# A retention block with a gated MLP on one core: two bit operations per float64 tile, a new order, and four half loads on ScalarE's queue

## The chip, the cores and the metric

The kernel runs on one core of a Trainium2 chip. The metric is the time of one execution on the device in microseconds. One core has a matrix engine (TensorE, PE in the profile, with its weight loads as PEld), three elementwise engines (VectorE as DVE, ScalarE as ACT, GpSimd as POOL), and a queue engine (SyncE, SP) that only issues transfers. Each engine runs its own instructions in program order; engines wait for one another and for transfers by semaphores. Transfers of all queues run on the core's 16 DMA engines.

## The reference

There are 4 batches, 8 heads, 768 positions and a head width of 64. The first part is retention, a linear attention with a decaying state, the second a gated MLP with a spatial gate:

```python
for t in range(S):
    state = gamma[None, :, None, None] * state + np.einsum('bhd,bhe->bhde', k[:, :, t], v[:, :, t])
    y[:, :, t] = scale * np.einsum('bhd,bhde->bhe', q[:, :, t], state)
# x: y with the heads side by side, [B, 768, 512]
h = x @ w_in                                             # [B, 768, 1024]
h = 0.5 * h * (1.0 + np.tanh(c * (h + 0.044715 * h ** 3)))
u, v = h[..., :512], h[..., 512:]
v_n = (v - mean(v)) / sqrt(var(v) + 1e-6) * g_ln
v_s = np.einsum('ts,bsd->btd', w_sg, v_n) + b_sg[None, :, None]
out = x + (u * v_s) @ w_out
```

`w_in` and `w_out` arrive as float64, all else as float32.

## The kernel before, in words

**Tiles and stages.** Positions are split in two halves of 384, each in six chunks of 64; heads go in four pairs. One attention unit (batch, half, pair) is written as three digits: 012 is batch 0, half 1, pair 2. There are 32 units. The MLP part runs on blocks of a batch and a half. Its matrix products are done in three passes of float32 in a reduced form: each operand is split into a high part and the rest, and high x high, high x rest and rest x high are summed.

**The order is written out by hand.** `PROG` is a string of some 1,200 words; a loop at the end reads it from left to right, and each word emits the instructions of one step. The order in which an engine sees its instructions is the order of the words that have work for it. The first letter names the step, digits its unit, and a last letter D, G or A the engine where there is a choice (VectorE, GpSimd, ScalarE). The steps that matter here:

- Attention: L loads a unit (`a_load`), P scales keys, S computes scores, D the states of the chunks, T scans the states (VectorE), M masks the scores (VectorE), W copies states beside them, K carries a state out and C carries it into the second half, O computes the output, X multiplies it out of PSUM (VectorE), H and I split it in a high part and the rest.
- MLP: V (four parts per block of 128 positions) and U (two parts) are the products with the two halves of `w_in`, v and u their activations; s and N (`v_rstd`, twelve small VectorE operations) make the normalization, n, a, b apply and split; G (three parts) is the product with `w_sg`, e (line 434) takes it out of PSUM, m gates, h and j split; Y is the product with `w_out`, r and y add the residual and store.
- Weights: a word with v, u, o or s and a number is a step for one of four tiles of `w_in`'s second half (v), of its first half (u), of `w_out` (o), or for one of twelve of `w_sg` (s). l loads. For the twelve float64 tiles (v, u, o), k (ScalarE) and b (VectorE) make a float32 from the upper 32-bit words, r (ScalarE) scales the lower words, a (GpSimd) adds them; h and o split the result.
- `~40` emits 40 filler matmuls on PE whose result nobody reads; R builds a table; Q loads the gate constants.

**Queues.** Every load and store goes through SP's queue except the first table, which ScalarE issues. An attention unit is three transfers: the keys (line 238, 384 KB on 128 partitions) and two halves of queries and values (line 247, 192 KB each, one on partitions 0 to 63, one on 64 to 127). A load waits until its buffer is free; the buffers of the units 000 to 003 are used for the first time there. Line 240 leaves out the second half for units that are in `ON_ACT`; a word Z (`a_load_rest`, line 249) then issues it from ScalarE's queue. `ON_ACT` is made of the Z words of `PROG` (line 106), and in the order before there is none.

**PSUM.** Two pools of four banks: one for attention (ds, sc, po), one for the MLP (pv, pu, ps, py, and the fillers). A matmul group that opens a tile waits until a bank of its pool has been read out.

Of the kernel before, what the change touches and what calls it, by code (L numbers as in the profile page):

```python
# [53 lines left out]
U0011 ko0 n001 a000 n002 U0031 bo0 a001 ko2 U0021 hs3A bo2 hs11A O013 u003 hs1A os3D D100 hs10A X013 b000G
u002 D101 H013A T100 S100 hs4A b001G hs2A S101 u001 M100 L102 ko1 K100 V0120 ko3 ao2 M101 V0110 L103 ro1 V0121
hs8A I013D a002 os1D V0111 Q hs6A os10D V0122 hs7A b002D W1001A U0101 os7D os4D P102A V0123 bo1 u010 V0112
v012 os8D V0100 W1000A s012 os2G V0113 T101 P103A V0101 ao1 v011 U0110 W1011A s011 K101 ho1A ao0 V0102 W1010A
U0120 os11D os6D V0103 bo3 U0130 v010 s010 ho0G U0121 N01 U0131 oo1G u012 U0111 u013 n011 n012 O100 u011 n010
ao3 D102 a010 X100 a011 O101 T102 H100A b010G D103 a012 ho2A S102 b012D S103 b011D L110 I100D G0020 M103 ho3G
L111 G0000 X101 C110 oo0G M102 C111 G0021 oo3D G0001 H101G G0022 P110A oo2D G0002 I101G V1020 K102 e000 W1021G  # L60
G0010 P111A m000D V1021 W1020G h000 G0011 j000D T103 r000G V1000 G0012 W1031A K103 W1030G V1001 e001 e002 O102
m001G D110 X102 m002G h001 O103 T110 D111 H102G h002 S110 W1100A j001D S111 W1101G M110 L112 G0030 M111 j002G
C113 L113 G0110 T111 I102G C112 G0031 W1110A r001D X103 r002G W1111A V1022 V1002 H103G G0032 P112G G0111 e003
I103D Y0000 m003G P113A V1023 h003 r003G V1003 v102 j003G G0112 s102 v100 s100 Y0001 G0100 y000 G0120 G0101
G0121 G0102 G0122 e010 e011 U1000 m010D m011D Y0010 r010D r011G U1001 G0130 u100 Y0020 Y0011 Y0021 y001 V1010
y002 G0131 Y0030 G0132 h010 h011 j010D Y0031 j011G e012 V1011 m012G y003 Y0110 e013 h012 r012G Y0130 j012D
Y0100 m013G V1012 h013 r013G O110 j013D D112 X110 O111 H110G T112 D113 S112 W1120A I110D S113 X111 W1121A L200
M112 H111A Y0111 I111G M113 L201 Y0131 y011 T113 Y0101 y013 W1131G Y0120 y010 W1130G V1013 Y0121 P200G v101
# [516 lines left out]
```

## Time and profile before

| | us |
|---|---|
| time, median of 3 runs | 412.82 (412.26 to 413.41) |
| the profiled execution's own time | 414.86 |
| its span, first to last instruction | 413.1 |
| busy: PE / PEld | 400.7 / 366.1 |
| busy: DVE / ACT / POOL | 247.1 / 146.6 / 155.2 |
| HBM read / written | 34.48 MB / 6.29 MB |

Times of the trace count from the first instruction. In rows of the timeline the first number is the start, the second the length, both in us; x24 is the number of instructions merged; brackets tell how long the engine idled before and what released it. In rows by line the busy time in us and the mean of one in ns follow the first bar, the idle time before and its releasers the second. A wait row is "engine line <- engine line waited for: us in total, times, longest us".

### The profile page before, as it was taken

To read this page: it belongs to the slowest core of one execution; us is meant where nothing else is said; L and a number is where in the kernel's file an instruction comes from. 1 tells how busy PE (TensorE), PEld (TensorE's weight loads), DVE (VectorE), ACT (ScalarE), POOL (GpSimd) and SP (SyncE) were. 2 spreads that over 40 slices of the span, in tenths; PEclk is the share of its full clock that TensorE was granted. 3 is DMA by queue.
4 is the path that set the end of the run, shared out by engine and by line. 5 is a ranking of instruction groups with operands and counts; after the bars stand their busy time and mean duration, and the time that the engine had idled before them with its cause. 6 is when DMAs were issued, how large, how long until landed. Compare 5 with 4: busy or idle time off the path is not lost.

```text
span 413.1 us, 9386 instructions
## 1 busy us (share of the span) xinstructions
PE 400.7 (97%) x3937; PEld 366.1 (89%) x3940; DVE 247.1 (60%) x488; ACT 146.6 (35%) x266; POOL 155.2 (38%) x161
## 2 busy tenths in 40 slices
PE   8998997999999999999999899999999999999996
PEld 3657886989999998999999898899998999899996
DVE  2799899987632674672761492741746855262652
ACT  4597687623411223442121152430234312230010
POOL 3446533638721530341651154230544133302421
PEclk9999999999999999999999999999999999999999
DMA  7999785032501070514042042500243210000012
GB/s 236 289 311 251 247 299 190 6 90 66 155 19 40 21 229 1 155 27 129 2 129 82 2 141 89 152 22 2 73 141 102 72 59 21 2 0 2 0 58 96
DMA packets 18123, 41.39 MB, mean 100 GB/s; under 512 B 2464, under 2 KB 8096, under 8 KB 18080
## 3 DMA queue, kind: packets, MB, share of 16 engines
q1 hardware_dynamic: 17936, 40.51, 32.6%
q8 instruction: 31, 0.51, 0.5%
q10 hardware_dynamic: 144, 0.27, 0.2%
q14 instruction: 12, 0.10, 0.1%
HBM read 34.48 MB, written 6.29 MB: 99 GB/s over the span
## 4 chain that ended last, share of the span: by engine, by line
PE 78%; DVE 9%; DMA 9%; issue 1%; ACT 1%; SPq 0%; ACTq 0%
PE ps L424 24%; PE py L462 16%; PE pv L351 13%; PE pu L407 13%; PE po L319 5%; DMA mw<-in_qv_dram 5%; PE sc L278 4%; PE ds L270 4%; DMA raw<-in_w_v_dram 2%; DMA tab<-in_c_tab_dram 1%; DMA raw<-in_w_sg_dram 1%; DVE ws L223 1%; DVE st L365 1%; DVE wx L187 1%; DVE mw L296 1%
## 5 line engine op out<-in xcount | busy, mean ns | idle before, releaser
L424 PE MATMUL ps<-ws,vh 128*128 128x384 f32 x576 | 105.7, 336 | 0.0
L424 PEld LDWEIGHTS ps<-ws,vh 128*128 128x128 f32 x576 | 100.6, 188 | 1.6
L407 PE MATMUL pu<-xh,wu 128*128 128x384 f32 x384 | 73.0, 339 | 1.6 <-DVE gt L434 1.1
L351 PE MATMUL pv<-wv,xh 128*128 128x512 f32 x288 | 74.1, 396 | 0.0
L462 PE MATMUL py<-gh,wo 128*128 128x384 f32 x384 | 72.1, 336 | 0.0
L407 PEld LDWEIGHTS pu<-xh,wu 128*128 128x128 f32 x384 | 67.5, 188 | 3.8 <-DVE gt L434 1.4
L462 PEld LDWEIGHTS py<-gh,wo 128*128 128x128 f32 x384 | 67.0, 188 | 0.7
L351 PEld LDWEIGHTS pv<-wv,xh 128*128 128x128 f32 x288 | 53.2, 188 | 9.5
L148 ACT COPY mw<-sq 64x320 f32<-64x320 f32 (+1 forms) x44 | 36.2, 822 | 29.9 <-DVE sq L283 29.6
L434 DVE SCALAR_TENSOR_TENSOR gt<-ps,gb 128x384 f32<-128x384 f32 x32 | 19.3, 612 | 43.8 <-PE ps L424 43.7
L449 ACT CAST gh<-gt 128x384 fp32r<-128x384 f32 x32 | 16.4, 514 | 74.5 <-POOL gt L445 31.3
L296 DVE TENSOR_TENSOR mw<-sc,tab 64x384 f32<-64x384 f32 x64 | 35.5, 555 | 9.4 <-PE sc L278 7.9
L365 DVE BATCH_NORM_STATS2 st<-v 128x6 f32<-128x512 f32 x24 | 16.4, 683 | 31.4 <-ACT v L361 31.4
L473 POOL TENSOR_TENSOR o<-xh 128x384 f32<-128x384 f32 x16 | 18.0, 1125 | 40.6 <-DVE gt L445 40.3
L326 DVE TENSOR_TENSOR x<-po,tab 128x384 f32<-128x384 f32 x32 | 17.6, 549 | 25.0 <-PE po L319 20.4
L278 PE MATMUL sc<-mw,kt 64*64 64x64 f32 x768 | 27.4, 219 | 5.1 <-DVE x L326 3.6
L477 DVE TENSOR_TENSOR o<-py,o 128x384 f32<-128x384 f32 x32 | 17.4, 552 | 25.0 <-PE py L462 24.9
L278 PEld LDWEIGHTS sc<-mw,kt 64*64 64x64 f32 x768 | 24.7, 135 | 8.0 <-DVE x L326 3.9
L283 DVE TENSOR_TENSOR_SCAN sq<-step,ds 128x384 f32<-128x384 f32 x32 | 30.1, 941 | 2.3 <-PE ds L270 1.6
L319 PEld LDWEIGHTS po<-mw 128*64 128x64 f32 (+1 forms) x768 | 26.2, 137 | 5.8 <-issue 3.7
L445 POOL TENSOR_TENSOR gt<-gt,u 128x384 f32<-128x384 f32 x18 | 19.2, 1071 | 31.7 <-DVE gt L434 31.7
L319 PE MATMUL po<-mw 128*64 128x64 f32 (+1 forms) x768 | 31.0, 226 | 0.0
(61 smaller groups left out, 420.2 us busy)
## 6 DMA issues: line engine op xcount, KB each, us to landing
kt<-in_kk_dram SPq DMA_DIRECT2D x32, 384.0 KB, 5.3
mw<-in_qv_dram SPq DMA_DIRECT2D x64, 192.0 KB, 5.3
out_dram<-o SPq DMA_DIRECT2D x32, 192.0 KB, 1.8
raw<-in_w_sg_dram SPq DMA_DIRECT2D x12, 192.0 KB, 7.2
raw<-in_w_v_dram SPq DMA_DIRECT2D x4, 512.0 KB, 7.2
raw<-in_w_u_dram SPq DMA_DIRECT2D x4, 512.0 KB, 8.6
raw<-in_w_out_dram SPq DMA_DIRECT2D x4, 512.0 KB, 7.6
gb<-in_gb_dram SPq DMA_DIRECT2D x1, 386.0 KB, 4.5
```

The source lines that it names most:

```text
L148: nc.scalar.copy(out=out, in_=in_)
L278: mm(out=scs[u][o, c], lhsT=kt[i, c], rhs=mv[j][i, c], start=True, stop=True)
L283: nc.vector.tensor_tensor_scan(out=sqs[u].rearrange("p e c -> p (e c)"), data0=step_t[:, p].rearrange("p e c -> p (e c)"), data1=dss.pop(u ...
L296: nc.vector.tensor_tensor(out=mv[j][h], in0=sc[h], in1=mask_t[h, p : p + 1, :].to_broadcast([64, NCH, C]), op=ALU.mult,)
L319: mm(out=pos[u][o, c], lhsT=w[j][i, c], rhs=mv[j][i, c], start=True, stop=True)
L351: mm(out=pv[b, hf, k], lhsT=x[:, p, a, k * 128 : (k + 1) * 128], rhs=wv_t[:, w, p], start=(p == 0 and n == 0), stop=(p == NP - 1 and n == 2),)
L365: nc.vector.bn_stats(out=st, in_=vt[b, hf, k])
L407: mm(out=pu[b, hf, f], lhsT=wu_t[:, w, f, p * 128 : (p + 1) * 128], rhs=x[:, p, a], start=(n == 0), stop=(n == 11),)
L424: mm(out=ps[b, hf, d], lhsT=vh[b, t][:, v, d * 128 : (d + 1) * 128], rhs=ws_t[hf * NT + t][:, w], start=(n == 0), stop=(n == 3 * NT - 1),)
L434: nc.vector.scalar_tensor_tensor(out=t, in0=ps.pop((b, hf, d)), scalar=g_t[:, d : d + 1], in1=b_t[:, hf * HT : (hf + 1) * HT], op0=ALU.mul ...
L445: engines[e].tensor_tensor(out=t, in0=t, in1=ut.pop((b, hf, d)), op=ALU.mult)
L462: mm(out=py[b, hf, c], lhsT=wo_t[c][:, w, d * 128 : (d + 1) * 128], rhs=gh[b, hf, d][:, a], start=(d == 0 and n == 0), stop=(d == 3 and n ...
```

## The change

The bits of a float64 are taken in another way. Before, k took the absolute value of the upper word read as a float32; b limited it from below (line 183), masked and shifted it left by three (line 184), and set the two upper bits from the original (line 187). After, k multiplies the upper word, read as a float32, by 2^-112, which moves its exponent; b shifts left by three and sets the sign bit from the original. Two VectorE operations stand where three stood, for each of the twelve tiles.

The order is written anew as a whole. It holds the same steps, apart from the fillers (40, 9, 8, 1 and 10 before; 40, 5, 3, 7, 1 and 1 after) and four new words Z000 to Z003. Some steps that have a choice move to another engine, in both directions. The beginning of the string and the places around N20:

```diff
-~40 lv0 R lv2 L000 lv3 L001 rv0 kv2 rv2 bv2 L010 kv0 bv0 P000A lu2 S000 av2 D000 M000 kv3 ~9 av0 rv3 T000 L011
-hv2A W0000A bv3 hv0A lv1 S001 P001A ov0D W0001A D001 ls10 ov2G M001 O000 lu0 av3 X000 P010A lu3 S010 H000A ~8
-K000 hv3A M010 ku2 ov3G T001 ru2 L002 C010 bu2 D010 W0011A ~1 P011A S011 I000D W0010A K001 L003 V0000 au2 M011
-C011 kv1 V0010 rv1 T010 V0020 hu2A bv1 W0100A D011 O001 ku0 ou2D L012 ~10 ru0 bu0 ru3 ku3 X001 av1 W0101A L013
-P002A S002 T011 H001G hv1A D002 M002 W0111A au0 O010 ls0 W0110A I001D hu0A S003 lo3 ov1D P003A O011 X010 ou0G
-lu1 T002 H010A D003 I010G M003 W0020A U0000 W0021A bu3 V0001 P012A V0021 X011 K002 au3 V0011 C012 T003 H011A
-P013A S012 W0030A I011D O002 W0031G M012 hu3A D012 ro3 K003 S013 X002 L100 C013 ou3D H002A O003 ku1 T012 I002G
+~40 L000 lv2 L001 lv3 lv0 lu2 R Z000 L010 kv2 rv2 bv2 Z001 av2 rv3 hv2A ov2D kv0 L011 rv0 bv0 ku2 kv3 P000G
+S000 L002 ru2 bu2 D000 ~5 bv3 lo3 T000 av0 P010A lu0 S010 P001A lu3 M000 S001 av3 W0000A D001 lv1 M010 hv0A ~3
+W0001A au2 M001 hv3A L003 O000 P011A K000 S011 ov3D C010 D010 T001 hu2G ~7 Z002 ov0G M011 W0011A W0010A X000
+K001 L012 ou2D ro3 O001 C011 T010 H000A D011 ku0 ~1 I000D ru0 bu0 V0000 ru3 V0010 W0100A X001 W0101G ls0 V0020
+H001A au0 T011 rv1 O010 L013 kv1 ~1 I001D ku3 S002 bv1 Z003 W0111A X010 W0110G M002 P002A av1 O011 H010A hu0A
+D002 P012A bu3 S012 hv1A S003 ls7 P003A ov1D lu1 T002 I010G V0011 Q ls3 V0001 M012 W0020A au3 V0021 W0021A
+X011 K002 M003 P013A D003 H011G hu3A O002 ou0G C012 T003 D012 ku1 S013 I011D L100 ru1 ou3D U0000 W0031A X002
...
-V2022 V2001 P213G V2023 V2002 v202 G1121 s202 U2000 V2003 U2001 v200 s200 U2010 u200 V2010 U2011 V2011 u201
-G1122 V2012 G1110 V2013 G1111 v201 s201 Y1030 N20 G1112 h110 j110G Y1031 e111 n202 U2020 e112 m111D O210 m112D
+G1120 s200 G1131 P213A G1110 G1132 G1111 V2010 G1112 V2011 e111 G1121 m111G V2012 r111D G1122 V2013 Y1030 v201
+s201 U2020 h110 h111 N20 j110G Y1031 j111G U2021 e112 O210 u202 e113 m112G D212 y103 O211 X210 m113G h112 T212
...
-    def w_abs(m, i):
+    def w_scale(m, i):
         hf = raw[m, i].bitcast(F32).rearrange("p (n t) -> p n t", t=2)[:, :, 1]
         x = wx[m, i] = act.tile([128, DF], F32, tag="gh", name="wx", bufs=4)
-        nc.scalar.activation(out=x, in_=hf, func=AF.Abs)
+        nc.scalar.activation(out=x, in_=hf, func=AF.Copy, scale=2.0**-112)
 
     def w_bits(m, i):
         hi = raw[m, i].bitcast(I32).rearrange("p (n t) -> p n t", t=2)[:, :, 1]
-        x = wx[m, i]
-        xi = x.bitcast(I32)
-        nc.vector.tensor_scalar(out=x, in0=x, scalar1=2.0**-15, scalar2=None, op0=ALU.max)
-        nc.vector.tensor_scalar(
-            out=xi, in0=xi, scalar1=0x07FFFFFF, scalar2=3, op0=ALU.bitwise_and, op1=ALU.logical_shift_left
-        )
+        xi = wx[m, i].bitcast(I32)
+        nc.vector.tensor_scalar(out=xi, in0=xi, scalar1=3, scalar2=None, op0=ALU.logical_shift_left)
         nc.vector.scalar_tensor_tensor(
-            out=xi, in0=hi, scalar=-0x40000000, in1=xi, op0=ALU.bitwise_and, op1=ALU.bitwise_or
+            out=xi, in0=hi, scalar=-0x80000000, in1=xi, op0=ALU.bitwise_and, op1=ALU.bitwise_or
         )
```

More of the change, by code (lines that the diff above doesn't have):

```diff
@@ L54 @@
[L54 to L68, printed above, removed]
@@ new lines @@
+ko2 os3D ls5 v001 V0023 bo2 v000 U0010 ls10 v002 s001 os0G H012A U0020 ro2 ls8 s002 I012G P101A U0100 s000
+W0130A ao2 U0030 N00 ko1 W0131G U0011 ko3 ro1 U0031 ko0 hs11G hs1A n000 U0021 u001 n001 a000 n002 a001 O013
+os1D a002 b000D D100 hs10A X013 b001G D101 hs5A T100 u003 S100 u002 H013G ro0 S101 b002D L102 W1000A os5D
+V0120 bo1 W1001A V0110 L103 bo0 V0121 V0111 ls2 bo3 V0122 M100 K100 V0112 I013G V0100 T101 os10G P102A V0123
+M101 W1011A U0101 K101 ao1 v012 V0113 W1010A s012 V0101 u010 os11G v011 U0110 ho1A s011 hs2G hs4A V0102 oo1G
@@ new lines @@
+hs8A hs6A U0120 hs7A os8D P103A V0103 os2D os7D U0130 v010 os6D os4G s010 U0121 N01 ao0 U0131 u012 ao3 U0111
+ho0A u013 O100 u011 n011 ho2A n012 D102 n010 O101 X100 ho3G a010 T102 D103 a011 oo2G a012 S102 H100A b012D
+S103 W1021A L110 b011D G0020 I100D M102 b010G L111 V1020 G0000 X101 C111 oo0G M103 C110 H101A G0021 I101D oo3G
+G0001 P110A G0022 K102 W1020G V1021 T103 G0002 W1031A K103 G0010 e000 P111A m000G W1030A G0030 r000D h000
+G0011 j000G G0031 G0012 G0032 e001 e002 m001G V1000 G0110 m002D h001 r001D h002 V1001 j001D j002G e003 G0111
@@ new lines @@
+O110 j012D D112 e013 O111 X110 m013G D113 T112 H110A S112 I110G h013 S113 M112 L200 j013G V1120 X111 W1120G
+U1021 L201 M113 H111A W1121G Y0110 u102 I111D r012D V1121 T113 r013G U1030 W1130A W1131G Y0111 P200A V1100
+y011 U1031 V1110 u103 P201A V1101 V1111 U1100 O112 D200 X112 O113 H112A T200 D201 I112G W2001A S200 K200 X113
+W2000A S201 M200 L202 H113A V1122 I113G T201 V1102 L203 M201 V1123 W2011A K201 V1103 W2010A V1112 v112 v110
+s112 Y0130 s110 V1113 P202A Y0120 v111 s111 Y0131 N11 Y0121 P203A Y0100 U1101 y013 n110 n111 Y0101 a110 n112
@@ new lines @@
+O301 H300A T302 D303 I300G W3020A S302 W3021G X301 S303 M302 L310 H301A K302 I301G G2000 C310 T303 C311 L311
+V3000 M303 W3030A W3031G G2001 K303 V3010 G2002 V3011 e200 P310G G2030 m200D h200 r200G G2010 j200D G2031
+P311G V3001 G2032 G2011 O302 D310 X302 O303 H302G T310 D311 I302D S310 W3100G X303 S311 M310 L312 H303A W3101G
+V3012 C313 I303G M311 C312 G2012 L313 T311 V3013 e201 V3002 W3110G v301 G2020 m201G s301 G2100 W3111G h201
+P312A j201D G2021 r201G V3003 G2022 v300 s300 P313A Y2020 e202 G2101 e203 m202G Y2030 m203D h202 r202D h203
@@ new lines @@
+Y2000 j202D j203G G2102 r203G Y2021 e210 m210G Y2031 y202 r210G Y2001 y203 Y2010 y200 G2110 h210 j210G Y2011
+G2120 y201 G2130 G2121 G2131 G2122 G2132 G2111 V3020 G2112 V3021 e211 e212 O310 m211G D312 X310 h211 r211G
+O311 T312 D313 H310G S312 W3121A m212D I310D S313 h212 r212D W3120A X311 j211G V3022 M313 H311A U3000 j212G
+T313 Y2130 I311D W3130A e213 W3131G V3023 M312 Y2120 m213G v302 s302 Y2100 h213 r213G N30 U3001 j213G O312
+u300 O313 n302 X312 Y2131 n301 H312A n300 Y2101 I312G y213 a300 a301 Y2121 b300D a302 X313 b301G V3120 y210
@@ L105 @@
+Y3021 Y3031 y302 r310D U3130 y303 G3112 U3131 e311 m311G G3120 u313 r311G Y3000 G3121 Y3010 G3122 h310 h311
+j310G Y3011 j311D Y3001 e312 e313 m312G Y3110 y301 y300 m313G h312 Y3130 j312D h313 Y3120 r312G Y3100 j313D
+r313D Y3111 Y3131 y311 Y3121 y313 Y3101 y312 y310
 """.split()
```

64 lines of the change are left out of this document (26 added, 38 removed).

## The prediction

> **What bounds the kernel now.** First the granted clock and the page's busy line, then three stretches of the span, cut at two matmul groups that stand in both orders: the scores of unit 012 (step S012) and the first product with the spatial weights (step G0020).
>
> ```profile
> core 0: 413.1 us, clock 1.000
> ...
> PE 400.7 (97%) x3937; PEld 366.1 (89%) x3940; DVE 247.1 (60%) x488; ACT 146.6 (35%) x266; POOL 155.2 (38%) x161
> ...
> 12.62:40.95 28.33, 25.80 (x427) 19.37 (x429) 25.54 (x43) 22.42 (x39) 15.01 (x15) 1.00 1.04 278
> 40.95:89.05 48.10, 44.00 (x569) 39.23 (x568) 43.54 (x91) 31.99 (x62) 21.16 (x22) 1.00 0.50 163
> 89.05:413.10 324.05, 319.47 (x2908) 303.04 (x2904) 173.75 (x348) 86.90 (x159) 114.29 (x117) 1.00 0.23 69
> ...
> 12.62 0.92 PE L278 MATMUL sc<-mw,kt 64*64 64x64 f32 x24
> ...
> 40.95 0.92 PE L278 MATMUL sc<-mw,kt 64*64 64x64 f32 x24
> ...
> 89.05 6.51 PE L424 MATMUL ps<-ws,vh 128*128 128x384 f32 x36
> ...
> 399.75 9.87 PE L462 MATMUL py<-gh,wo 128*128 128x384 f32 x56
> ```
>
> A window's row gives its length, then the busy time of PE, weight loads, DVE, ACT and POOL, clock, DMA share and GB/s. PE is the engine to shorten, at full clock. The last stretch has 4.58 us without a matmul, of which 3.48 lie behind the last one (399.75 + 9.87 = 409.62, to 413.10); 1.1 is a stall. So what can be won lies in the first 89 us: 2.53 us idle in the first stretch, 4.10 in the second, and the filler matmuls in front of expected waits. What ends those waits is told by the waits of PE, and by DVE ahead of the longest one:
>
> ```profile
> PE sc L278 <- DVE x L326: 3.6, 2, 2.9
> PE sc L278 <- DMA mw<-in_qv_dram: 1.3, 3, 0.5
> ...
> PE pu L407 <- DVE gt L434: 1.1, 1, 1.1
> PE pu L407 <- ACT v L361: 0.5, 1, 0.5
> ...
> 7.88:89.05 81.17, 73.05 (x140) 1.00 0.72 210
> ...
> 60.19 0.42 DVE L183 TENSOR_SCALAR wx<-wx 128x512 f32<-128x512 f32 x1
> ...
> 63.64 0.41 DVE L183 TENSOR_SCALAR wx<-wx 128x512 f32<-128x512 f32 x1
> ...
> 65.62 0.55 DVE L326 TENSOR_TENSOR x<-po,tab 128x384 f32<-128x384 f32 x1
> ...
> 66.23 0.91 PE L278 MATMUL sc<-mw,kt 64*64 64x64 f32 x24 [2.91 <-DVE x L326]
> ```
>
> DVE is 90% busy from its first weight operation to G0020 (73.05 of 81.17), and PE's longest stall, 2.91 us, ends on a DVE multiply that stood behind the bit operations of two weight units. In the first stretch the DMA engines are full instead (share 1.04), and PE waits for units to land.
>
> **The two operations.** Twelve weight units pass through these groups:
>
> ```profile
> L196 ACT ACTIVATE raw<-raw 128x512 int32<-128x512 uint32 x12 | 8.1, 672 | 6.7 <-DMA raw<-in_w_out_dram 3.6 <-DMA raw<-in_w_v_dram 3.0
> L175 ACT ACTIVATE wx<-raw 128x512 f32<-128x512 f32 x12 | 7.9, 668 | 3.3 <-DMA raw<-in_w_v_dram 3.3
> ...
> L183 DVE TENSOR_SCALAR wx<-wx 128x512 f32<-128x512 f32 x12 | 7.3, 611 | 6.8 <-ACT wx L175 6.8
> L184 DVE TENSOR_SCALAR wx<-wx 128x512 int32<-128x512 int32 x12 | 7.1, 588 | 0.4
> ```
>
> Line 183 goes: 12 x 0.611 = 7.3 us of DVE, all of it ahead of G0020, where DVE is the fullest engine. Line 184 loses one of its two steps. The page has no single-step shift; its nearest rows are 588 ns with two steps and 611 with one, so I take no change, with 12 x 0.02 us either way. ScalarE's Abs (668 ns) becomes a Copy with a scale, which line 196 already is (672): +0.05 us in all, taken as nothing, since ACT has 5.9 of 28.33 us free even in the fullest stretch.
>
> **The loads.** The second halves of units 000 to 003 move to ScalarE's queue. The unit that sets S012 lands late in a stretch of full DMA engines:
>
> ```profile
> kt<-in_kk_dram SPq DMA_DIRECT2D x32, 384.0 KB, 5.3
> mw<-in_qv_dram SPq DMA_DIRECT2D x64, 192.0 KB, 5.3
> ...
> raw<-in_w_u_dram SPq DMA_DIRECT2D x4, 512.0 KB, 8.6
> ...
> 23.00:26.90 3.90, 3.88 (x43) 2.85 (x43) 3.48 (x7) 3.41 (x7) 1.50 (x1) 1.00 1.03 412
> 27.00:36.00 9.00, 7.33 (x146) 5.43 (x144) 8.71 (x14) 7.87 (x13) 4.56 (x4) 1.00 1.05 237
> ...
> 0.72 0.40 ACTq L481 DMA_DIRECT2D tab<-in_c_tab_dram  x1
> ...
> 28.49 2.00 SPq L247 DMA_DIRECT2D mw<-in_qv_dram  x2
> ...
> DMA to landing us min/median/max: 8.3/8.7/9.0
> ```
>
> The last row is the landing of the two issues at 28.49, the halves of unit 012: the second, issued at about 30.0, is down 9.0 us later, at 39.0. The issue order puts weights into the first of the two DMA windows (412 GB/s) and attention units into the second (237 GB/s), and half of a unit's bytes goes to 64 partitions at a time (lines 245 to 247). Counting sizes in issue order, unit 012 is complete on SP after 9152 KB before and 9280 after; the latter holds 320 KB more of weights and leaves out the half of 003 that stands behind it in ScalarE's order. That is 0.8 us more (320 KB at 412 GB/s) and 0.8 less (192 KB at 237), so 39.0 again, if the other queue changes nothing. The three halves that are issued from ScalarE ahead of that point are worth 0.83 us each (192 KB at 237 GB/s) if they run beside other traffic: 2.5 us, and 36.5. I take 36.5, because the engines have shown 412 GB/s on full-width traffic and a stream that mixes both partition halves is nearer to that than one half after the other; 39.0 stays as the other end.
>
> The Trainium skill speaks against me: SBUF — State Buffer, section "Can I just issue two DMAs to hit both halves?", says that two concurrent transfers to the two partition halves serialize on the same 16 engines, with a gain of only 6%. The 237 GB/s row agrees with slow halves in one queue; no run here shows them in two. By that rule S012 stays at 39.0, the first rival's case.
>
> What else ScalarE pays: four issues of 0.40 us, by the table's row, 1.6 us, covered by those 5.9 idle us; without that cover they cost 1.6 us. SP is passed the other way: its queue now begins with unit 000, with the weights v0 behind two more units' starts, covered by the 40 fillers that hold PE until 12.62 in both.
>
> **The order.** Ahead of S012 stand 17 fillers besides the first 40 instead of 28, and five groups of work go behind it: the scores and states of 003, one half of a U group and three V groups.
>
> ```profile
> 28.42 2.11 PE L492 MATMUL wp<-warm 128*128 128x512 bf16 x9 [0.16 <-issue]
> ...
> 35.09 0.91 PE sc L278 x22
> ...
> 36.85 0.84 PE ds L270 x24
> 37.69 1.24 PE pu L407 x6
> 38.93 2.09 PE pv L351 x9
> ```
>
> The moved groups are 0.91 + 0.84 + 1.24 + 2.09 = 5.1 us. Ten fillers (one record is missing) take 2.11 us, so 11 fewer are 2.3 us. PE's own work up to S012 shrinks from 25.80 to 25.80 - 5.1 - 2.3 = 18.4 us; it could be there at 31.0 with no wait, at 33.5 with the waits of before (2.53). Landing at 36.5 comes later and decides. The fillers are thus no gain by themselves: they are wait of another name.
>
> From S012 to G0020 PE has 44.00 + 5.1 = 49.1 us of work. Of the 4.1 us idle there, 3.6 ended on DVE; five of the twelve weight units lie in this part (5 x 0.611 = 3.05 us less on DVE), so 0.55 of it stays, with the 0.5 that ended on ACT: 1.1. G0020 then comes at 36.5 + 49.1 + 1.1 = 86.7 instead of 89.05: 2.35 us.
>
> Behind G0020 the matmuls are the same. The 1.1 us stall stands at N20:
>
> ```profile
> 233.06 0.17 DVE L375 TENSOR_SCALAR lna<-mvar 128x3 f32<-128x3 f32 x1
> ...
> 236.01 0.61 DVE L434 SCALAR_TENSOR_TENSOR gt<-ps,gb 128x384 f32<-128x384 f32 x1
> ...
> 236.68 1.31 PE L407 MATMUL pu<-xh,wu 128*128 128x384 f32 x6 [1.10 <-DVE gt L434]
> ```
>
> Line 434 waits behind the twelve small operations of N20 (233.06 to 236.01), and a U group for the bank that it frees. The new order puts U2020 and that release ahead of N20, with the next new bank six attention groups later. I take the 1.1 us as won and no new stall; if another stall of its kind opens, nothing is won, and this is the unknown cost, 0 to 2.2 us.
>
> Sum: 413.1 - 2.35 - 1.1 = 409.65 of span. The profiled execution took 414.86 us; the median is 2.04 lower, at 412.82. Taken from it: 412.82 - 3.45 = 409.4.
>
> **Rivals.** (1) The halves serialize in two queues as in one. S012 at 39.0, G0020 at 39.0 + 49.1 + 1.1 = 89.2, nothing won in front, 1.1 behind: 411.9. For it: DMA share 1.04, full already. Against: the 237 beside 412 GB/s.
>
> (2) DVE alone sets the front. Then its 7.3 us come out whole, 8.4 with N20: 404.4. For it: 73.05 of 81.17 us busy; S012 could be reached at 31.0, and loads that land by 33 would show it. Against: before S012 DMA is full and PE's waits there end on landings.
>
> (3) Slower: Z003 is late. In ScalarE's order this issue stands behind both activations of weight v1, whose load is complete after 7744 KB. Before, unit 002 was complete after 7616 KB, and its scores waited for the landing until 31.73:
>
> ```profile
> 31.73 0.85 PE L278 MATMUL sc<-mw,kt 64*64 64x64 f32 x21 [0.46 <-DMA mw<-in_qv_dram]
> ```
>
> So v1 lands near 32, and with three activations of 0.67 Z003 is issued at 34. If it lands as slowly as SP's halves (9.0), S003 waits until 43, and behind it are 49.1 - 0.9 us of PE work: G0020 at 43 + 48.2 + 1.1 = 92.3, 3.2 later, less 1.1: 414.9. It decides from a landing 5.7 us behind the issue (39.75 + 49.3 = 89.05). For it: the in-order queue. Against: SP's 9.0 us contain its own backlog, and ScalarE's queue has none.
>
> (4) The new order gains nothing from fewer DVE operations, as PE finds other waits: between (1) and 412.8, held in (1).
>
> **Chances.** Forecast 0.48, own range 407.4 to 411.3; (1) 0.17; (2) 0.20; (3) 0.15. About 0.3%, 1.2 us, is what a measurement can tell from no change. Faster: 0.47 of the forecast, all of (2) and 0.06 of (1), 0.73; same: 0.01, 0.10 of (1) and 0.03 of (3), 0.14; slower: 0.13. The range reaches near (2) and half way into (3): 404.8 to 413.6.
>
> **What would show it.** DVE 5 to 8 us less busy, with two groups of 12 on the weights' bits; 57 fillers; S012 near 36.5 with a DMA landing as its releaser, G0020 near 86.7; no PE wait of 2 us on DVE; under 4 us without a matmul behind G0020. Wrong: S012 at 39 or later (rival 1), S003 released by a half on ScalarE's queue (rival 3), or a stall of over 2 us behind G0020, which no step here foresees.

## The result, and the profile after

The changed kernel takes 425.53 us (median of 4 executions, 422.18 to 427.13) against 413.12 us (412.26 to 414.95): 1.0249 of before, 95% interval 1.0204 to 1.0294. It is slower by 10 to 12 us where 3.4 us less was forecast. Its profiled execution took 426.16 us, with a span of 424.2.

The busy line and the granted clock on the page of the changed kernel:

```profile
PE 404.1 (95%) x3925; PEld 368.9 (87%) x3929; DVE 248.8 (59%) x472; ACT 144.5 (34%) x267; POOL 158.8 (37%) x164
...
PEclk9989799998999999999999999999999999999999
```

DVE has 16 instructions fewer (472 for 488) and is busy 1.7 us longer (248.8 for 247.1). The clock, full throughout before, dips in three places. The stretches of the changed kernel, cut at the same two steps, and three tens with a dip:

```profile
12.49:37.20 24.71, 19.31 (x352) 14.84 (x355) 21.13 (x34) 17.86 (x33) 11.90 (x12) 0.93 1.04 290
37.20:97.77 60.57, 52.45 (x638) 46.19 (x634) 50.11 (x92) 35.51 (x67) 32.93 (x33) 0.92 0.47 139
97.77:424.20 326.43, 321.06 (x2906) 303.47 (x2904) 176.17 (x344) 87.95 (x164) 108.59 (x111) 1.00 0.22 69
...
20.00:30.00 10.00, 8.49 (x150) 6.21 (x148) 9.82 (x16) 7.65 (x15) 5.52 (x7) 0.83 1.04 320
...
40.00:50.00 10.00, 6.84 (x83) 5.61 (x85) 3.93 (x7) 3.99 (x7) 2.02 (x3) 0.66 0.44 131
...
90.00:100.00 10.00, 6.88 (x116) 6.05 (x112) 9.19 (x20) 2.83 (x5) 5.59 (x5) 0.83 0.22 70
```

The first stretch ends 3.75 us earlier than before (37.20 for 40.95). The second is 12.47 us longer (60.57 for 48.10), the third 2.38 (326.43 for 324.05): 11.1 us of span in all. Single microseconds inside these dips show 0.50, so a mean of 0.66 over 10 us means that some 6.8 us of them ran at half clock, 0.83 means 3.4 us. PE around those dips:

```profile
17.92 0.30 PE L276 MATMUL sc<-mw,kt 64*64 64x64 f32 x2 [2.62 <-DMA mw<-in_qv_dram]
...
36.44 0.92 PE L268 MATMUL ds<-mw,kt 64*64 64x64 f32 x24
37.20 1.17 PE L276 MATMUL sc<-mw,kt 64*64 64x64 f32 x26
43.16 1.54 PE L276 MATMUL sc<-mw,kt 64*64 64x64 f32 x22 [4.79 <-DMA mw<-in_qv_dram]
44.63 3.60 PE L349 MATMUL pv<-wv,xh 128*128 128x512 f32 x9
...
95.08 2.76 PE L276 MATMUL sc<-mw,kt 64*64 64x64 f32 x48 [3.05 <-DVE x L324]
97.77 1.70 PE L422 MATMUL ps<-ws,vh 128*128 128x384 f32 x6
...
100.40 0.50 PE L349 MATMUL pv<-wv,xh 128*128 128x512 f32 x1 [0.47 <-DVE xh L336]
```

S012 (37.20; the 26 matmuls are its 24 and the first two of S003) follows the states ahead of it without a wait. Right behind it PE waits 4.79 us for unit 003, and the nine V matmuls behind that wait take 3.60 us, where the prediction's row has 2.09. At 95.08 the scores S102 wait 3.05 us for a bank that DVE empties. The first of the two ends on the half that ScalarE issues; ScalarE's timeline:

```profile
32.21 1.25 ACT L178 ACTIVATE wx<-raw 128x512 f32<-128x512 f32 x2
34.17 0.47 ACTq L245 DMA_DIRECT2D mw<-in_qv_dram  x1
```

and the landing of that one issue (its size in KB, then us to landing):

```profile
mw<-in_qv_dram ACTq DMA_DIRECT2D x1, 192.0 KB, 8.9
```

34.17 + 8.9 = 43.07: the first score of S003 begins at 43.16. The second wait has DVE in front of it, first on four splits of spatial weights, then on N01 (89.69 to 93.10), its scalings, and only then the multiply X100 that empties the bank:

```profile
83.43 5.41 DVE L221 TENSOR_TENSOR ws<-raw,ws 128x384 fp32r<-128x384 f32 x4 [0.43 <-ACT ws L149]
...
89.69 1.21 DVE L373 TENSOR_SCALAR lna<-mvar 128x3 f32<-128x3 f32 x1
...
93.10 1.46 DVE L385 TENSOR_SCALAR v<-v,mvar,lny 128x512 f32<-128x512 f32 x3
94.47 0.55 DVE L324 TENSOR_TENSOR x<-po,tab 128x384 f32<-128x384 f32 x1
```

The four splits take 1.35 us each. GpSimd works beside them, on its timeline:

```profile
83.91 1.33 POOL L221 TENSOR_TENSOR ws<-raw,ws 128x384 fp32r<-128x384 f32 x1
85.20 3.23 POOL L200 TENSOR_TENSOR wx<-wx,raw 128x512 int32<-128x512 int32 x2
```

DVE's groups show where its saving went:

```profile
L336 DVE TENSOR_TENSOR xh<-x,xh 128x384 fp32r<-128x384 f32 x15 | 11.9, 792 | 0.0
...
L185 DVE SCALAR_TENSOR_TENSOR wx<-raw,wx 128x512 int32<-128x512 int32 x12 | 9.4, 782 | 0.4
...
L221 DVE TENSOR_TENSOR ws<-raw,ws 128x384 fp32r<-128x384 f32 x8 | 7.7, 993 | 0.4 <-ACT ws L149 0.4
L184 DVE TENSOR_SCALAR wx<-wx 128x512 int32<-128x512 int32 x12 | 7.0, 586 | 9.2 <-ACT wx L178 9.2
```

The weights' bits are two groups of 12 now. Before, the same splits of xh took 559 ns each (14 of them) and those of the spatial weights 741 (9); here 792 and 993. In these two groups alone DVE is busy 5.4 us longer than before (11.9 for 7.8 and 7.7 for 6.4), of the 7.3 us saved.

### The profile page after: what moved, and what is told of

It reads as the page before. It is cut to its first block, busy times and chain, and to the rows that moved or that the text cites. A ratio compares the mean times of both kernels' runs of the same rounds, so it can differ in the third digit from the quotient of the medians.

```text
span 424.2 us, 9359 instructions
## 1 busy us (share of the span) xinstructions
PE 404.1 (95%) x3925; PEld 368.9 (87%) x3929; DVE 248.8 (59%) x472; ACT 144.5 (34%) x267; POOL 158.8 (37%) x164
## 4 chain that ended last, share of the span: by engine, by line
PE 75%; DVE 11%; DMA 10%; issue 2%; ACT 2%; SPq 0%; DVEq 0%; ACTq 0%
PE ps L422 22%; PE py L460 15%; PE pv L349 13%; PE pu L405 12%; DMA mw<-in_qv_dram 8%; PE po L317 5%; PE ds L268 4%; PE sc L276 4%; DVE ws L221 2%; DMA raw<-in_w_v_dram 1%; DVE vh L395 1%; DVE v L385 1%; DVE xh L336 1%; DVE st L363 1%; DVE sq L281 1%
## 5 line engine op out<-in xcount | busy, mean ns | idle before, releaser
L422 PE MATMUL ps<-ws,vh 128*128 128x384 f32 x576 | 107.3, 337 | 0.0
L349 PE MATMUL pv<-wv,xh 128*128 128x512 f32 x288 | 78.5, 404 | 0.5 <-DVE xh L336 0.5
L405 PE MATMUL pu<-xh,wu 128*128 128x384 f32 x384 | 74.6, 339 | 0.8 <-DVE gt L432 0.5
L460 PEld LDWEIGHTS py<-gh,wo 128*128 128x128 f32 x384 | 67.1, 188 | 2.4 <-DVE gt L432 1.3
L349 PEld LDWEIGHTS pv<-wv,xh 128*128 128x128 f32 x288 | 53.7, 191 | 10.4 <-DVE xh L336 1.4
L443 POOL TENSOR_TENSOR gt<-gt,u 128x384 f32<-128x384 f32 x20 | 20.5, 1033 | 81.9 <-DVE gt L432 81.8
L149 ACT COPY mw<-sq 64x320 f32<-64x320 f32 (+1 forms) x41 | 33.0, 806 | 35.4 <-DVE sq L281 33.9
L276 PE MATMUL sc<-mw,kt 64*64 64x64 f32 x768 | 28.5, 228 | 10.9 <-DMA mw<-in_qv_dram 7.9
L276 PEld LDWEIGHTS sc<-mw,kt 64*64 64x64 f32 x768 | 26.1, 142 | 12.7 <-DMA mw<-in_qv_dram 5.5
L415 ACT ACTIVATE u<-pu 128x384 f32<-128x384 f32 x32 | 15.6, 491 | 58.4 <-PE pu L405 58.3
L336 POOL TENSOR_TENSOR xh<-x,xh 128x384 fp32r<-128x384 f32 x17 | 17.7, 1041 | 45.1 <-ACT xh L149 44.5
L324 DVE TENSOR_TENSOR x<-po,tab 128x384 f32<-128x384 f32 x32 | 17.6, 549 | 24.5 <-PE po L317 22.1
L151 POOL COPY mw<-sq 64x384 f32<-64x384 f32 (+1 forms) x23 | 21.2, 922 | 24.6 <-DVE sq L281 12.5
```

The costliest lines, as they stand in the source:

```text
L149: nc.scalar.copy(out=out, in_=in_)
L151: engines[e].tensor_copy(out=out, in_=in_)
L276: mm(out=scs[u][o, c], lhsT=kt[i, c], rhs=mv[j][i, c], start=True, stop=True)
L336: engines[e].tensor_tensor(out=t[:, p, 1], in0=xs.pop((b, hf, p)), in1=t[:, p, 0].bitcast(F32), op=ALU.subtract)
L349: mm(out=pv[b, hf, k], lhsT=x[:, p, a, k * 128 : (k + 1) * 128], rhs=wv_t[:, w, p], start=(p == 0 and n == 0), stop=(p == NP - 1 and n == 2),)
L405: mm(out=pu[b, hf, f], lhsT=wu_t[:, w, f, p * 128 : (p + 1) * 128], rhs=x[:, p, a], start=(n == 0), stop=(n == 11),)
```

## The experiments

Ratios are to the kernel before, run beside each on the same chip (medians there 414.15 to 414.8 us). G0020 and the rest are the profiled execution's: where the first product with the spatial weights begins, and the span from there. The diffs show the words around each move; the rest of a line is left out.

| | edit | median us | ratio [95%] | G0020 / rest |
|---|---|---|---|---|
| after | | 425.53 | 1.0249 [1.0204, 1.0294] | 97.8 / 326.4 |
| e1 | before + two operations | 412.83 | 0.9963 [0.9931, 0.9996] | 87.3 / 324.4 |
| e6 | e1 + Z behind each L | 412.87 | 0.9959 [0.9931, 0.9987] | 89.0 / 324.0 |
| e2 | after without Z | 422.42 | 1.0180 [1.0101, 1.0258] | 95.7 / 326.7 |
| e3 | after, Z002, Z003 early | 420.07 | 1.0125 [1.0072, 1.0179] | 91.2 / 326.8 |
| e4 | after, more fillers | 425.98 | 1.0276 [1.0224, 1.0327] | 95.8 / 326.5 |
| e7 | e1 without small fillers | 412.01 | 0.9942 [0.9909, 0.9976] | 85.1 / 324.2 |
| e9 | e1 without two of them | 413.90 | 0.9961 [0.9927, 0.9995] | 87.9 / 324.3 |
| e5 | e3, GpSimd's work later | 419.46 | 1.0132 [1.0092, 1.0172] | 88.9 / 330.1 |
| e8 | e3, engines of before | 418.52 | 1.0102 [1.0064, 1.0140] | 90.4 / 325.9 |
| e12 | e3, L010 earlier | 422.80 | 1.0165 [1.0115, 1.0215] | 93.4 / 327.4 |
| e10 | front of e3, tail of before | 416.76 | 1.0042 [1.0009, 1.0075] | 89.5 / 325.2 |
| e11 | front of e1, tail of after | 417.05 | 1.0058 [1.0023, 1.0093] | 86.4 / 328.0 |
| e13 | e10, N01 behind X100 | 416.57 | 1.0054 [1.0028, 1.0080] | 89.5 / 326.3 |
| e17 | e10, N01 behind D103 | 414.39 | 1.0006 [0.9987, 1.0025] | 85.1 / 326.5 |
| e15 | e11, V1020 later | 414.67 | 1.0027 [0.9998, 1.0056] | 86.4 / 325.8 |
| e16 | e3, both moves (e13, e15) | 418.18 | 1.0103 [1.0077, 1.0129] | 90.1 / 326.8 |
| e18 | e3, both moves (e17, e15) | 418.28 | 1.0086 [1.0057, 1.0115] | 85.6 / 331.2 |
| e14 | e1, two waits mended | 413.31 | 0.9970 [0.9951, 0.9990] | 88.3 / 324.5 |

**The two operations alone (e1).** The order of before, with the new k and b:

```diff
-        nc.scalar.activation(out=x, in_=hf, func=AF.Abs)
+        nc.scalar.activation(out=x, in_=hf, func=AF.Copy, scale=2.0**-112)
...
+        nc.vector.tensor_scalar(out=xi, in0=xi, scalar1=3, scalar2=None, op0=ALU.logical_shift_left)
```

> The order of before, its fillers and its queues; only k and b are those of the change (one VectorE operation less for each of the twelve tiles). Theory: the bits are sound and the loss comes from loads and clock, so this runs 1 to 5 us faster than before (408 to 412 us), VectorE about 7 us less busy, clock 1.00. Rival (the new bit operations themselves cost, or the freed VectorE time collides with GpSimd): within 1 us of before or slower.

Measured 0.9963: 1.5 us won (0.2 to 2.9). DVE's two groups in e1:

```profile
L184 DVE SCALAR_TENSOR_TENSOR wx<-raw,wx 128x512 int32<-128x512 int32 x12 | 10.2, 853 | 0.4
L183 DVE TENSOR_SCALAR wx<-wx 128x512 int32<-128x512 int32 x12 | 8.6, 716 | 6.9 <-ACT wx L177 6.9
```

Together 18.8 us, where three groups took 23.7 (7.3 + 7.1 + 9.3). So 4.9 us of DVE go, not 7.3, and the end moves by a third of that. The operations are not what makes the changed kernel slow.

**The loads on ScalarE's queue (e2, e3, e6).** e2 takes the Z words out, so all halves are on SP's queue; e3 keeps them and issues 002 and 003 right behind their other transfers:

```diff
-lu2 R Z000 L010 kv2 rv2 bv2 Z001 av2
+lu2 R L010 kv2 rv2 bv2 av2
...
-hu2G ~7 Z002 ov0G
+hu2G ~7 ov0G
...
-ku3 S002 bv1 Z003 W0111A
+ku3 S002 bv1 W0111A
```

```diff
-S000 L002 ru2 bu2
+S000 L002 Z002 ru2 bu2
...
-hv3A L003 O000
+hv3A L003 Z003 O000
...
-hu2G ~7 Z002 ov0G
+hu2G ~7 ov0G
...
-ku3 S002 bv1 Z003 W0111A
+ku3 S002 bv1 W0111A
```

> The changed kernel with the four Z words taken out: all halves on SP's queue, all else as changed. Theory (the half of unit 003 on ScalarE's queue lands at 43 and holds PE, and the idle time halves the clock): the scores of 003 come before 41 us, the half-clock stretch from 40.6 to 47.4 is shorter or gone, the time falls by 3 to 8 us against the changed kernel (417 to 422). Rival (the new order as such, with its place for unit 012 and its fewer fillers, loses whatever the queue): 424 or more.

> The changed kernel with Z002 and Z003 issued from ScalarE's queue directly behind the word that loads the rest of their unit, in front of the activations that wait for weights. Theory: the place in ScalarE's order made the half late, not the queue: the half of 003 is issued near 22 us in place of 34 and is down before 37; PE does not wait at the scores of 003, and the time falls by 4 to 8 us (417 to 421). Rival (transfers on ScalarE's queue are late by themselves): the scores of 003 wait until 40 or later, and the time stays within 2 us of the changed kernel.

e3 is 5.1 us faster than the changed kernel by the ratios (5.5 by the medians): that is the price of Z's place in ScalarE's queue, and the two intervals do not meet. e2 lies between them, and its interval overlaps both; its theory is missed by little (S003 only behind 41.65 us where 41 was expected, 422.42 us for 417 to 422). e3's waits on PE:

```profile
18.03 0.29 PE L276 MATMUL sc<-mw,kt 64*64 64x64 f32 x2 [3.25 <-DMA mw<-in_qv_dram]
...
37.08 1.61 PE L276 MATMUL sc<-mw,kt 64*64 64x64 f32 x46 [0.41 <-DMA mw<-in_qv_dram]
...
88.94 2.35 PE L276 MATMUL sc<-mw,kt 64*64 64x64 f32 x48 [3.05 <-DVE x L324]
```

The same places in e2, with the loads all on SP:

```profile
20.52 3.24 PE L276 MATMUL sc<-mw,kt 64*64 64x64 f32 x47 [4.72 <-DMA mw<-in_qv_dram]
...
41.65 1.61 PE L276 MATMUL sc<-mw,kt 64*64 64x64 f32 x46 [0.29 <-DMA mw<-in_qv_dram]
```

The last matmuls of S012 and those of S003 run at 37.08 in e3 and at 41.65 in e2, in both behind a landing. In the same order of steps, the loads with four halves on a second queue are 4.6 us further on. S010 is 2.5 us later in e2 already, also behind a landing. From 2 to 37 us the DMA engines, full in both, moved 10.70 MB in e3 and 9.59 in e2.

e6 puts Z into the order of before, behind each L:

```diff
-lv2 L000 lv3 L001 rv0
+lv2 L000 Z000 lv3 L001 Z001 rv0
...
-ru2 L002 C010
+ru2 L002 Z002 C010
...
-K001 L003 V0000
+K001 L003 Z003 V0000
```

> The order and fillers of before, the new bits, and the second halves of 000 to 003 from ScalarE's queue, each Z word directly behind its L word. Theory (halves on two queues run side by side): the scores of 002 and 003 wait no longer for landings, unit 012 is down 2 to 4 us earlier than 39, and the time falls to 408 to 411 us, 1 to 3 us under the kernel with the new bits alone. Rival (halves serialize, or VectorE holds the front anyway): within 1 us of the bits alone, 412 to 414.

0.9959 is e1 again, the rival's case. Z takes away the waits on unit 002 and 003, and another opens in e6:

```profile
25.27 0.80 PE L267 MATMUL ds<-mw,kt 64*64 64x64 f32 x20 [3.40 <-ACT ds L258]
```

In this order the second queue brings nothing forward: 10.11 MB moved from 2 to 37 us where e1 has 10.16, and the second half of unit 012, issued at 32.2, is down 6.5 us later at 38.7, where the theory had 35 to 37. So that halves on a second queue land earlier is shown for the new order and not for the old one; what decides it is open. The Trainium skill, SBUF — State Buffer, section "Can I just issue two DMAs to hit both halves?", has two such transfers serialize, with a gain of 6%: e6 against e1 agrees, and e3 against e2, 12% more bytes in the same time, does not.

**Clock and fillers (e4, e7, e9).** e4 fills the changed kernel's two longest waits for loads with matmuls that nobody reads; e7 and e9 take fillers out of e1, all four small groups or the last two:

```diff
-D000 ~5 bv3
+D000 ~17 bv3
...
-S012 hv1A S003
+S012 hv1A ~22 S003
```

```diff
-M000 kv3 ~9 av0
+M000 kv3 av0
...
-S010 H000A ~8
+S010 H000A
...
-W0011A ~1 P011A
+W0011A P011A
...
-L012 ~10 ru0
+L012 ru0
```

```diff
-W0011A ~1 P011A
+W0011A P011A
...
-L012 ~10 ru0
+L012 ru0
```

> The changed kernel with more fillers ahead of its two longest load waits: 17 in place of 5 before the scores of 010, and 22 new ones before the scores of 003; the loads and all else as changed. Theory (idle time halves PE's clock and the slow work behind it costs time): granted clock 1.00 up to 90 us, the landings unmoved, the time 2 to 4 us below the changed kernel (421 to 424). Rival (fillers only fill a wait, the clock costs nothing): the same time as the changed kernel, or up to 2 us more.

> The order of before with the new bits, and the 28 fillers behind the first 40 taken out; nothing else. Theory (idle time of 2 us and more halves the granted clock for 3.4 us or a multiple): a half-clock stretch appears between 14 and 40 us, and since loads and VectorE hold this part, the time rises by 0 to 3 us over the bits alone (412 to 416). Rival (the fillers hold PE up): 1 to 4 us faster than the bits alone.

> The order of before with the two new operations, and the filler groups of 1 and 10 matmuls behind unit 011 and behind L012 left out (fillers compute nothing that the output needs). Theory: behind these fillers PE waits little (no wait over 0.4 us on a landing between 30 and 36 us of the span), so leaving them out brings G0020 from 87.3 to about 85 with the clock full throughout, and 412.8 us becomes 410.6 to 411.8. Rival (the prediction's sentence that fillers are wait of another name): the landings set the scores of unit 012, PE waits as long as the fillers lasted, G0020 stays at 87 and the time at 412.5 to 413.

e4 has the clock back and not the time: 425.98. The ten microseconds with S003, in e4:

```profile
40.00:50.00 10.00, 10.00 (x174) 7.97 (x174) 5.81 (x9) 3.22 (x7) 3.74 (x4) 1.00 0.34 109
```

Full clock, and 10 us busy, part of it with fillers. S102 begins at 93.23 in e4's profile, 1.85 us earlier than in the changed kernel, and waits for DVE exactly as long (3.05 us). The median does not follow. In e9, PE without its last fillers meets a wait on DVE that was hidden, and nothing is won:

```profile
30.48 0.44 PE L275 MATMUL sc<-mw,kt 64*64 64x64 f32 x2 [2.53 <-DVE x L323]
```

e9's theory is wrong. As the rival said, G0020 stays (87.9) and the ratio is e1's, though the wait ends on DVE and not on a landing: a filler there is wait of another name. e7 is 0.8 us below e1 by the medians, with overlapping intervals, so no gain over e1 is shown. Its theory was half right: the mean clock is 0.85 from 10 to 20 us and 0.81 from 20 to 30 in e7's profile, and the time did not rise.

**DVE beside GpSimd (e5, e8).** e5 moves six steps on GpSimd and on ScalarE behind S102; e8 gives each step of e3 the engine that it had before:

```diff
-U0121 N01 ao0 U0131 u012 ao3 U0111
-ho0A u013
...
-X100 ho3G a010
...
-a011 oo2G
+U0121 N01 U0131 u012 U0111
+u013
...
+X100 a010
...
+a011 oo2G
...
+X101 C111 ao0 ao3
...
+H101A ho0A ho3G
...
+I101D oo0G oo3G
```

```diff
-kv3 P000G
+kv3 P000A
...
-T001 hu2G
+T001 hu2A
...
-X001 W0101G
+X001 W0101A
...
```

> The kernel with Z002 and Z003 early, and the sums and splits of w_out's tiles 0 and 3 (ao0, ao3, ho0A, ho3G, oo0G, oo3G) moved behind X101, so that GpSimd no longer works on them while VectorE splits w_sg. Theory (VectorE operations with two inputs in SBUF stretch while GpSimd works, and this delays N01, X101 and the scores of 102): the splits of w_sg ahead of N01 fall from 1.35 to about 0.6 us each, the wait of 3.05 us ahead of the scores of 102 shrinks to under 1, and the time falls by 2 to 4 us against the kernel with early halves (416 to 418). Rival (the wait comes from where N01 stands in the order): the wait stays at 2.5 us or more and the time within 1 us.

> The kernel with Z002 and Z003 early, its new order kept, but every step with a choice of engine on the engine it had before. Theory (the new order's places, by which VectorE and GpSimd work at the same time and N01 stands late, cost it, not the choice of engines): within 2 us of the kernel with early halves (418 to 422). Rival (the moved steps cost VectorE its gain): VectorE 4 us or more less busy and the time 3 to 6 us lower (414 to 417).

In e5 the waits move instead of going:

```profile
87.21 1.77 PE L276 MATMUL sc<-mw,kt 64*64 64x64 f32 x48 [0.88 <-DVE x L324]
...
92.29 0.73 PE L349 MATMUL pv<-wv,xh 128*128 128x512 f32 x2 [2.06 <-ACT xh L149]
93.68 0.53 PE L349 MATMUL pv<-wv,xh 128*128 128x512 f32 x1 [0.66 <-DVE xh L336]
```

S102 waits 0.88 instead of 3.05, G0020 comes at 88.9, and V1020 behind it pays; the median is e3's within the intervals. The splits of spatial weights did get shorter, 714 ns on average for 991 in e3, so the theory had the collision right and its price wrong. In e8, DVE is busy 241.4 us where e3 has 249.4, with four operations more (476 for 472), and S102's wait falls to 1.66; the time falls by 1.5 us, with overlapping intervals, inside the theory's range; of the rival only the lower busy time came. So the collision of DVE and GpSimd is there, some 8 us of busy time, and no gain from undoing it is shown beyond the intervals.

**The front or the tail (e10, e11).** Each joins one order up to G0020 with the other behind it:

```diff
-b011D G0020 I100D M102 b010G L111 V1020 G0000
+b011D b010G I100D G0020 M103 L111 G0000 X101
...
```

```diff
-I100D G0020 M103 ho3G L111 G0000 X101 C110
+I100D ho3G oo2G W1021A G0020 M102 L111 V1020 G0000 X101 C111
...
```

> The program with Z002 and Z003 early (420.1 us) up to G0020; all words behind it in the order of before, on the engines that they have there. Theory, that the new order loses 2.4 to 2.7 us behind G0020 in its own right: G0020 stays near 91 and the rest falls from 326.8 to about 324.3, in all 417 to 418. Rival, that what is lost behind G0020 is only debt of the front (DVE and ACT late when PE gets there): the rest stays near 326.5 and the time near 420.

> The order of before, with the two new operations, up to G0020; all words behind it in the new order. Theory, that the new order loses behind G0020 in its own right: G0020 near 87.3, the rest 326 to 327 instead of 324.4, in all 414.5 to 415.5. Rival, that it is debt of the new front: the rest at 323.5 to 324.5 (the stall at N20 gone), in all 411.5 to 413.

The new front alone is 0.79 points above e1, 3.3 us; the new tail alone 0.95 points, 3.9 us. The sum, 7.2, is the distance of e3 to e1, 6.7, within the intervals. So the tail is no debt of the front. In e10 the rest falls to 325.2, most of the way to its theory's 324.3. e11 came out slower than its theory had it (rest 328.0 for 326 to 327). Its wait is V1020's, PE's next group behind G0020:

```profile
90.60 0.50 PE L348 MATMUL pv<-wv,xh 128*128 128x512 f32 x1 [2.37 <-DVE xh L335]
```

In the order of before, V1020 stands behind six groups of the spatial product.

**S010's landing (e12).** L010 ahead of two weights:

```diff
-L001 lv3 lv0 lu2 R Z000 L010 kv2
+L001 lv3 L010 lv0 lu2 R Z000 kv2
```

> The program with Z002 and Z003 early (420.1 us), and L010 moved ahead of lv0, lu2, R and Z000 on SP's queue. Theory, that the 3.25 us wait of S010 and the half clock behind it (18.2 to 21.6) cost the front what they last, because PE sets the end there: the wait falls under 1.5 us, the clock stays full there, G0020 comes 2 to 4 us earlier (87 to 89) and the time is 416 to 418. Rival, that DVE and GpSimd set the front of the new order: S010 comes early, S102 still waits for the multiply that DVE makes, now longer (4 to 6 us), G0020 stays at 90.5 to 91.5 and the time at 419.5 to 420.5.

Slower than e3 by 2.7 us by the medians, which neither side expected; the intervals overlap. S010's long wait is gone, and PE waits behind it:

```profile
22.61 1.54 PE L268 MATMUL ds<-mw,kt 64*64 64x64 f32 x24 [5.79 <-DVE sq L281]
```

In DVE's order the scan that releases it stands behind bit operations of weights, and these now wait for ScalarE:

```profile
17.18 0.43 DVE L184 TENSOR_SCALAR wx<-wx 128x512 int32<-128x512 int32 x1 [3.89 <-ACT wx L178]
...
21.52 0.95 DVE L281 TENSOR_TENSOR_SCAN sq<-step,ds 128x384 f32<-128x384 f32 x1
```

ScalarE in turn waits 3.92 us for a landing of `w_in` there. L010 went ahead in full DMA engines, a load of `w_in` came late, and DVE, which keeps its order, carried that lateness to a scan that needs neither. PE's mean clock from 18 to 29 us is 0.53 in e12, so the run does not tell what S010's wait alone costs.

**The named steps (e13, e15 to e18, e14).** e13 moves N01 with its scalings behind X100, e17 behind T102 and D103 as well (T102 is the scan that the expectations mean; D103 is a step of PE); e15 moves V1020; e16 and e18 do both on e3:

```diff
-u011 n011 ho2A n012 D102 n010 O101 X100 ho3G
+u011 ho2A D102 O101 X100 N01 n011 n012 n010 ho3G
```

```diff
-n010 O101 X100 ho3G a010 T102 D103 a011
+O101 X100 ho3G T102 D103 N01 n011 n012 n010 a010 a011
```

```diff
-L111 V1020 G0000
+L111 G0000
...
-P110A G0022 K102
+P110A G0022 V1020 K102
```

> The program with the new front and the tail of before (416.8 us), with the normalisation N01 and its three scalings n011, n012, n010 moved on VectorE behind X100. Theory, that S102's 3.05 us wait comes from X100 standing behind these 15 instructions (81.8 to 86.6 us of the span) on VectorE: the wait falls under 0.5 us, G0020 comes 2 to 3 us earlier (86.5 to 87.5 instead of 89.5), the half clock behind it goes, and the time is 412.8 to 414.5. Rival, that VectorE is late altogether by then: another wait for VectorE or ScalarE, on the products of unit 01 or behind G0020, takes its place, and the time stays at 416 to 417.

> The program with the front of before and the new tail (417.05 us), with V1020 moved behind G0022, three groups of spatial products later. Theory, that the new tail's largest loss is its third matmul, which waits 2.37 us for the low part of xh that VectorE makes only then (88.9 to 90.6): the wait falls under 0.3 us, the rest behind G0020 from 328.0 to 325.5 to 326, the time to 414.4 to 415.2. Rival, that PE only meets the same late VectorE at the next product: a wait of 1.5 us or more stands at V1020's new place or at V1021, and the time stays at 416.5 to 417.5.

> The program with Z002 and Z003 early (420.1 us), with both moves: N01, n011, n012, n010 behind X100, and V1020 behind G0022. Theory, that the named waits are what the new order loses behind 45 us of the span: S102's wait (3.05 us) falls under 0.5 us, no wait over 1 us stands behind G0020, and the time falls to 415 to 417; what is left over before is S010's wait with its half clock and the two waits on the gate offsets. Rival, that the new order is late on VectorE by its load beside GpSimd: other waits for VectorE open at once, 418.5 to 420.

> The program with the new front and the tail of before (416.8 us), with N01, n011, n012, n010 and a010 moved behind D103 as well as behind X100, so that neither the multiply X100 nor the scans D102 and D103, which S102 and S103 wait for, stand behind the 15 operations of the normalisation on VectorE. Theory, that S102's wait is the place of N01: no wait of S102 or S103 over 0.5 us, G0020 at 86.5 to 87.5 instead of 89.5, 412.8 to 414.5 us. Rival, that VectorE is late altogether: another wait of over 1.5 us for VectorE or ScalarE between 75 and 110 us of the span, and 416 to 417 us.

> The program with Z002 and Z003 early (420.1 us), with N01, n011, n012, n010 and a010 behind D103, and V1020 behind G0022. Theory, that these two places are what the new order loses behind 45 us of the span: no wait over 1 us there, the rest behind G0020 at 324.5 to 325.5, 414.5 to 416.5 us in all; what is left over before is S010's wait with its half clock. Rival, VectorE late altogether: a wait of over 1.5 us at another place behind 75 us, 417.5 to 419 us.

e15 is the clearest: the wait is gone, and the median falls from 417.05 to 414.67, in the range of its theory (0.31 points by the ratios, whose intervals overlap). e13 left the scan T102 behind N01 and got nearly the same wait from it:

```profile
88.05 1.55 PE L275 MATMUL sc<-mw,kt 64*64 64x64 f32 x24 [2.75 <-DVE sq L280]
```

e17 mends that: 416.76 to 414.39 against e10, 0.36 points, again with overlapping intervals. S102's wait is gone, so it was N01's place. Part of it comes back, since the spatial product needs what N01 normalizes; e17's rows:

```profile
83.61 1.57 PE L275 MATMUL sc<-mw,kt 64*64 64x64 f32 x48
85.11 3.23 PE L421 MATMUL ps<-ws,vh 128*128 128x384 f32 x17
88.88 1.84 PE L421 MATMUL ps<-ws,vh 128*128 128x384 f32 x9 [0.55 <-POOL vh L394]
```

On the whole new order (e16, e18) the two moves bring 1.8 to 1.9 us by the medians (0.22 and 0.39 points, inside the intervals), nearer to the rivals than to the theories: e18 begins G0020 at 85.58, 5.6 us before e3, and loses 4.4 of that behind it, first here:

```profile
95.55 1.35 PE L348 MATMUL pv<-wv,xh 128*128 128x512 f32 x3 [1.89 <-ACT xh L148]
```

e14 mends the two DVE waits that e1 has left:

```diff
-U0031 bo0 a001 ko2 U0021 hs3A bo2 hs11A
+U0031 a001 ko2 U0021 hs3A hs11A
...
-hs10A X013 b000G
+hs10A X013 bo0 bo2 b000G
...
-Y1030 N20 G1112
+Y1030 G1112
...
-Y1031 e111 n202
+Y1031 e111 N20 n202
```

> The order of before with the two new operations (0.9963 of before), with the bit operations bo0 and bo2 moved on VectorE behind X013, and the normalisation N20 behind the offset e111. Theory: these are the two VectorE waits left on PE's path (1.57 us at 65.4, 1.09 us at 235.4), what stood ahead of the awaited operation is not urgent, so both waits go and the time falls by about 2.6 us, to 0.990 of before (409.5 to 411). Rival: the moved operations are as late for the next reader, PE waits as long elsewhere, and the ratio stays at 0.995 to 0.998.

The rival's case: 0.9970. In e1 PE waits 1.6 us in all for the multiply of line 323 and 1.1 at N20; in e14 it waits 2.7 for that multiply, in three places. N20's wait now stands at S202, 1.14 us, for the multiply behind the moved N20:

```profile
240.17 1.77 PE L275 MATMUL sc<-mw,kt 64*64 64x64 f32 x48 [1.14 <-DVE x L323]
```

e1, e6, e7, e9 and e14 beat both kernels, by 0.3 to 0.6%; none of them beats e1 beyond its interval.

## Why the prediction was wrong

The forecast span was 409.65 us, the profiled one 424.2. By the cuts: S012 +0.7 (37.20 for 36.5), the stretch from there to G0020 +10.4 (60.57 for 50.2), the rest +3.5 (326.43 for 322.95).

- **S012 at 36.5** came out near, 37.20, but not for the reason given. The forecast has PE there at 33.5 and lets the landing of unit 012 decide. PE came there at 37.20 by itself: 19.31 us of work for 18.4, and 5.40 us idle for 2.53, of which 3.10 (2.62 and 0.48) behind S010's landing, which no term of the sum prices. The landing came at the same time: the half of 012 issued at 27.93 is down 9.5 us later, at 37.4. That the two meet is luck; in e3 the landing does decide (37.08). In the kernel before, S012 began without a wait too, at 40.95, two us after its unit was down at 39.0. Rival (1)'s 39.0 did not come true; its rule is open, since e2 against e3 speaks against it and e6 for it.
- **The loads of 003: the step that failed first.** Rival (3) had the mechanism and the moment: Z003 issued "at 34" (34.17), a landing of 9.0 (8.9), S003 "until 43" (43.16). It got 0.15 because "SP's 9.0 us contain its own backlog, and ScalarE's queue has none". For this issue that was wrong: it landed as late as SP's. But a sooner landing would not have saved it: 6.7 us, the landing of Z002, the ScalarE issue before it, gives 40.9, still behind the 39.75 from which rival (3) decides. In the forecast's own sum, the groups that moved behind S012 (six, where it says five) were counted as work (5.1 us) without asking when the first of them could begin. The rival's price was near: 414.9 is 5.5 us above the forecast, and after against e3 gives 5.1. The rest of the way to 425.53 lies in other steps.
- **The clock**, which no step considered, since every row of before showed 1.00. PE's busy time from S012 to G0020 is 52.45 us for 49.1 forecast, 3.35 us more, with two stretches at half clock in it. Whether they cost that much of the end is not shown: e4 had full clock behind S003's wait and no better time, and e7 has half clock and is not slower than e1.
- **"1.1 idle" in that stretch** was 8.12 (60.57 - 52.45): 4.79 at S003 and 3.05 at S102. The forecast took 3.05 us of fewer DVE operations off the waits on DVE, one for one. e1 shows the exchange: 4.9 us of DVE for 1.5 us of time. The new order has N01 ahead of the multiply that PE waits for, as before has it, but DVE gets there later: X100 at 94.47 and at 86.75 before (in e1 at 84.97).
- **The 7.3 us of line 183** went as counted, and line 184 at 586 ns stayed at "no change" in the changed kernel (716 in e1). That the other DVE rows would stay as they were was assumed without a row; the new order put splits beside GpSimd, and DVE's sum rose.
- **"The 1.1 us as won and no new stall"**: N20's stall is gone, and 0.47, 0.47 and 0.90 us opened elsewhere. The unknown cost was bounded at 2.2 us; the new tail costs 3.9 against that of before (e11), of which V1020 is 1.3 (e15, by ratios with overlapping intervals). Of the other 2.6 us the profile of e15 names 1.4 at most (rest 325.8 for e1's 324.4); the cause of what is left stays open.
- **The front of the new order** costs 3.3 us with Z002 and Z003 early (e10). N01's place is 1.5 of it (e17, by ratios with overlapping intervals); of the other 1.8 S010's wait for its landing is the likeliest part, which no run shows by itself.
- **"Fillers are wait of another name"** held in e4 and e9.

In all, by the ratios: -1.5 us for the operations, +3.3 for the new front, +3.9 for the new tail (6.7 for both together), +5.1 for Z's place: 10.3 us. Rival (2), DVE alone sets the front, is nearest in kind behind 45 us, with the sign turned: DVE set it, and was later.

## What to carry to other kernels

A transfer that is moved to an engine's queue starts when that engine comes to it: work out the issue time from what stands ahead of it, add the landing that a neighbour shows in full DMA engines, and ask for the first step that needs it, not only for the step that was the latest so far. Busy time saved on an engine in order is worth what it moves the one operation that somebody waits for; look up what stands ahead of that operation, and where the operation behind it then waits. A whole new order is tested in halves: join the old front with the new tail, and the other way round, before explaining either.
